# A recurrent attention with memory beside plain attention, on one core: the recurrence's value projection in four column tiles, its late rows in one early batch, its softmax sums by a matmul of ones and ln/exp

## The chip, the cores and the metric

The kernel runs on one core of a Trainium2 chip. The metric is the device time of one execution in microseconds (us). TensorE (PE) does the matmuls, VectorE (DVE) and ScalarE (ACT) the element-wise work, GpSimd (POOL) helps, SyncE (SP) issues DMAs.

## The reference

Two branches read the same x (2048 rows of 576) and are mixed by a gate. Branch A is a recurrence over 64 segments of 32 rows: 8 memory rows and 32 rows of x form h (40 rows); the memory rows of the output are the memory of the next segment. Branch B is full attention over all 2048 rows with 32 heads of 18.

```python
# A: 32 heads of 128, M = 8 memory rows, seg = 32, L = 40
mem = mem0
for s in range(64):
    h = concatenate([mem, x[:, s*32:(s+1)*32]], axis=1)       # 40 x 576
    q, k, v = h@Wq, h@Wk, h@Wv                                # 32 heads x 40 x 128
    p = softmax(where(mask, q@k.T * scale, -1e9))             # mask: key is memory, or not later
    o = (p @ v) @ Wo                                          # 40 x 576
    mem, a[s] = o[:, :8], o[:, 8:]
# B: plain softmax attention over 2048 rows, 32 heads of 18, then @ wo
g = sigmoid((x * gate_w).sum(-1))
out = g * a + (1 - g) * b
```

## The kernel before

**Opening.** x is loaded, transposed to `xT`, and B's queries, keys and values are projected (L164, L183) and written to DRAM. Then the weights of A are loaded: `wq`, `wk`, `wv` (4096 columns in five chunks of rows of Dm, the fifth padded with zeros) and `wo`.

**Recurrence.** Each segment does the following, in this order of dependence: x of the segment is transposed (L336) into columns 8 to 39 of `ht`; Q and K are projected head by head, five 128x40 matmuls each (`proj_T`, L351, 160 for Q and 160 for K); V in eight banks of 512 columns, five matmuls each (`v_part`, L371, 40 in all, 40 useful rows of a 128-wide stationary); scores with a mask matmul (L393, L402) and exp on ScalarE (L409); the row sums by 32 one-column matmuls (L417), reciprocal, a diagonal matrix (L425) and 32 matmuls that spread it (L436), and the multiplication (L443); then values times probabilities (L454), the output projection of 160 matmuls (L470, tile `pbw`), two casts that put the new memory in `ht_next` (L482, L483), and the transposed output (L491).

**Branch B fills in.** `b_steps` yields 512 steps, one per group of four heads, query block of 512 and key block of 128. A step is four score matmuls (L255, tile `sb`, each in its own 32-row tile of the array), two exps of 128x1024 on ScalarE (L267, `etb`), and four value matmuls (L270, tile `ob`, each in its own 32-column tile). `b_advance(per_seg)` adds 8 steps after each segment; a scheduler places the instructions on each engine in a fixed order, and each engine then runs its own in that order. PSUM holds three one-bank buffers that all of A's tiles share in turn (tag `pb`), two two-bank buffers for `sb` and one for `ob`.

**Closing.** b's output projection, the gate and the sum, 16 blocks of 128 rows (L525 to L543).

## Time and profile before

| what | value |
|---|---|
| median of 3 runs | 3181.43 us (3160.13 to 3200.14) |
| the profiled execution | 3178.58 us, its span 3176.8 us |
| PE busy | 3024.0 us, 95% of the span |
| ACT busy | 1481.7 us, 47% |
| DVE busy | 813.6 us, 26% |
| mean granted TensorE clock | 0.826 |

A busy PE is not a PE at its peak: a row of matmuls counts as busy from the first start to the last end. What one matmul costs in a run of them is read from start to start in a list in order of time.

### The profile page before, as it was taken

Reading aid. Unit: us, or ns where it says so; the run is one execution under the profiler, and the core shown is the slowest. Engines: PE = TensorE matmul, PEld = TensorE weight load, DVE = VectorE, ACT = ScalarE, POOL = GpSimd, SP = SyncE. Lnnn points to the kernel's source line nnn. Section 1 sums busy time; section 2 is a strip of 40 time slices with the busy share of each in tenths; the row PEclk is TensorE's granted clock in tenths of the full one; section 3 lists DMA queues with packets and bytes.
Section 4 is the critical chain, followed back from the end, with each engine's and each line's share of the span. In section 5 each row is a group of like instructions: output and inputs, shape, how many; then the busy total and the mean of one; then the engine's idle time right before and its main releaser. Section 6 shows DMA issues by size and latency. Waiting matters only on the chain.

```text
span 3176.8 us, 101992 instructions
## 1 busy us (share of the span) xinstructions
PE 3024.0 (95%) x47622; PEld 1807.9 (57%) x47765; DVE 813.6 (26%) x1664; ACT 1481.7 (47%) x2206; POOL 33.7 (1%) x144
## 2 busy tenths in 40 slices
PE   6789999999999999999999999999999999999996
PEld 3446555566556556555555655566565656565653
DVE  5312222222222222122222212222222222222214
ACT  2353445454544554454545445454544454445440
POOL 0100000000000000000000000000000000000000
PEclk9868887898879888787878878798888888788878
DMA  5640000000000000000000000000000000000004
GB/s 120 174 185 4 6 6 25 5 4 6 5 24 6 6 6 25 4 6 5 5 26 6 5 4 6 24 6 6 5 25 3 6 5 6 24 6 6 5 3 124
DMA packets 91117, 73.60 MB, mean 23 GB/s; under 512 B 63676, under 2 KB 82820, under 8 KB 88964
## 3 DMA queue, kind: packets, MB, share of 16 engines
q1 hardware_dynamic: 62210, 54.16, 5.5%
q10 hardware_dynamic: 28482, 12.90, 1.7%
q8 instruction: 373, 6.11, 0.8%
q14 instruction: 52, 0.43, 0.0%
HBM read 45.54 MB, written 21.50 MB: 21 GB/s over the span
## 4 chain that ended last, share of the span: by engine, by line
PE 88%; ACT 6%; DMA 3%; DVE 1%; issue 1%; ACTq 0%; SPq 0%; DVEq 0%
PE pb L351 19%; PE pvv L371 18%; PE ob L270 13%; PE sb L255 13%; PE pbw L470 11%; ACT etb L267 5%; PE pso L454 3%; PE psh L393 3%; PE psn L436 3%; PE psh L402 2%; PE pq L164 2%; PE psums L417 1%; DMA otn<-otd 1%; DMA wq<-in_A_Wq_dram 1%; PE po L525 1%
## 5 line engine op out<-in xcount | busy, mean ns | idle before, releaser
L267 ACT ACTIVATE etb<-sb 128x1024 bf16<-128x1024 f32 x1024 | 1011.0, 1024 | 385.2 <-PE sb L255 370.3
L371 PE MATMUL pvv<-wv,ht 128*128 128x512 bf16 x2432 | 583.3, 386 | 7.4 <-issue 1.2
L270 PE MATMUL ob<-etb,vgi 128*32 128x512 bf16 x2048 | 527.3, 471 | 55.0 <-ACT etb L267 49.4
L255 PE MATMUL sb<-qtg,ktg 18*128 18x512 bf16 x2048 | 537.4, 465 | 0.0
L351 PEld LDWEIGHTS <-wq 128*128 128x128 bf16 x10240 | 315.5, 99 | 185.8 <-issue 185.8
L371 PEld LDWEIGHTS <-ht 128*128 128x128 bf16 x2560 | 243.1, 99 | 287.7 <-issue 26.0
L351 PE MATMUL pb<-ht,wq 128*128 128x40 bf16 x10240 | 382.2, 185 | 15.4 <-DMA wq<-in_A_Wq_dram 15.4
L381 ACT CAST v_sb<-pvv 40x512 bf16<-40x512 f32 x256 | 148.0, 578 | 509.7 <-PE pvv L371 509.7
L470 PEld LDWEIGHTS <-wo 128*128 128x128 bf16 x10240 | 336.8, 109 | 39.1 <-issue 34.5
L470 PE MATMUL pbw<-qt_sb,wo 128*128 128x40 bf16 x10240 | 352.1, 195 | 0.0
L379 DVE CAST v_sb<-pvv 40x512 bf16<-40x512 f32 x256 | 174.8, 683 | 445.3 <-PE pvv L371 445.3
L351 PEld LDWEIGHTS <-wk 128*128 128x128 bf16 x10240 | 268.7, 96 | 15.2
L351 PE MATMUL pb<-ht,wk 128*128 128x40 bf16 x10240 | 269.6, 180 | 0.1
L255 PEld LDWEIGHTS <-ktg 18*128 18x128 bf16 x2048 | 106.9, 94 | 264.7 <-issue 255.7
L361 DVE CAST qt_sb<-pb 128x320 bf16<-128x320 f32 x128 | 62.9, 492 | 623.2 <-PE pb L351 617.4
L270 PEld LDWEIGHTS <-vgi 128*32 128x32 bf16 x2048 | 121.6, 95 | 168.9 <-issue 122.8
L486 ACT CAST ots<-pbw 128x128 bf16<-128x128 f32 x64 | 17.0, 265 | 311.6 <-DVE ht L483 251.3
L443 DVE TENSOR_TENSOR kt_sb<-psn,kt_sb 40x320 bf16<-40x320 f32 x256 | 111.8, 475 | 73.1 <-PE psn L436 72.6
L409 ACT ACTIVATE kt_sb<-psh 40x320 bf16<-40x320 f32 x256 | 110.0, 430 | 40.0 <-PE psh L402 16.5
L361 DVE CAST kt_sb<-pb 128x320 bf16<-128x320 f32 x128 | 62.9, 492 | 253.1 <-PE pb L351 253.1
L454 PEld LDWEIGHTS <-v_sb 40*128 40x128 bf16 x2048 | 79.8, 107 | 75.9 <-issue 75.0
L363 ACT CAST kt_sb<-pb 128x320 bf16<-128x320 f32 x128 | 54.4, 425 | 129.9 <-PE pb L351 129.9
(81 smaller groups left out, 1638.9 us busy)
## 6 DMA issues: line engine op xcount, KB each, us to landing
wo<-in_A_Wo_dram SPq DMA_DIRECT2D x1, 4608.0 KB
qtd<-stg SPq DMA_DIRECT2D x8, 512.0 KB, 4.3
qtg<-qtd SPq DMA_DIRECT2D x8, 512.0 KB, 3.6
ktd<-stg SPq DMA_DIRECT2D x8, 512.0 KB, 4.4
vgd<-vg ACTq DMA_DIRECT2D x8, 512.0 KB, 3.5
ktg<-ktd SPq DMA_DIRECT2D x8, 512.0 KB, 4.8
vgi<-vgd SPq DMA_DIRECT2D x8, 512.0 KB, 4.9
wq<-in_A_Wq_dram SPq DMA_DIRECT2D x1, 4096.0 KB
```

What stands on the lines that cost most here:

```text
L255: nc.tensor.matmul(sb[:, i, :], lhsT=ktg[32 * j:32 * j + DhB, kb * P:(kb + 1) * P], rhs=qtg[32 * j:32 * j + DhB, qc * QC:(qc + 1) * QC], s ...
L267: nc.scalar.activation(out=etb[:, :, :], in_=sbs[jp][:, :, :], func=ACT.Exp, scale=scale_b)
L270: nc.tensor.matmul(ob[32 * j:32 * j + 32, :], lhsT=vg[:, kb * P + 32 * j:kb * P + 32 * j + 32], rhs=ets[j // 2][:, j % 2, :], start=(kb == 0),
L351: nc.tensor.matmul(pb[:, 64 * j:64 * j + L], lhsT=w_tile[0:cz, c, h * Dh:(h + 1) * Dh], rhs=ht[0:cz, c, :], start=(c == 0), stop=(c == NC ...
L361: nc.vector.tensor_copy(out=dst, in_=src)
L371: nc.tensor.matmul(ph[:, 0:512], lhsT=ht_flat[0:cz, L * c:L * c + P], rhs=wv[0:cz, c, q8 * qcols:(q8 + 1) * qcols], start=(c == 0), stop=( ...
L379: nc.vector.tensor_copy(out=v_sb[0:L, q8 * qcols:(q8 + 1) * qcols], in_=ph[0:L, :])
L381: nc.scalar.copy(out=v_sb[0:L, q8 * qcols:(q8 + 1) * qcols], in_=ph[0:L, :])
L409: nc.scalar.activation(out=vw(et[0:L, HS * h0:HS * (h0 + 8)], HS, L), in_=vw(psh[0:L, :], 64, L), func=ACT.Exp, scale=scale_a,)
L443: nc.vector.tensor_tensor(out=vw(et[0:L, HS * h0:HS * (h0 + 8)], HS, L), in0=vw(psn[0:L, :], 64, L), in1=vw(et[0:L, HS * h0:HS * (h0 + 8)] ...
L454: nc.tensor.matmul(pso[:, 64 * j:64 * j + L], lhsT=v_sb[0:L, h * Dh:(h + 1) * Dh], rhs=et[0:L, HS * h:HS * h + L], start=True, stop=True,)
L470: nc.tensor.matmul(pbwv[0:cz, c, 0:L], lhsT=wo[:, h, c * P:c * P + cz], rhs=ot_sb[:, HS * h:HS * h + L], start=(h == 0), stop=(h == H - 1),)
```

## The change

The kernel computes the same and its tiling of B and its closing stay. What is different:

- **Values.** Of the 40 rows of V, the first 32 are computed in the segment, by 40 matmuls with a 32-column stationary and 512 moving columns, four of which (j = 0 to 3) write to four different 32-partition strips of one bank (L403). Two casts to `vm` and four DMAs bring them to `v_sb`. The last 8 rows of all 64 segments depend on x alone: they are computed in the opening in one batch (L248, 160 matmuls), go to DRAM (`vld`), and each segment loads its 8 rows (L389).
- **Q and K.** 576 is four chunks of 128 and a half one of 64. The half chunks of two heads share one 128-row stationary, so 16 matmuls of 80 columns (L430) take the place of 32 of 40, and 128 of 40 columns stay (L421). Banks hold 12, 12 and 8 heads.
- **Softmax.** The mask is a minimum with `cap` on VectorE (L458) behind the exp. One matmul of ones per bank sums and spreads in one (L465); ln (L476) and exp of its negative (L478) on ScalarE make the reciprocal, and VectorE multiplies it with `pso` (L479). Stationaries are padded to 128 rows and columns.
- **x.** Transposed once, in the opening, written to DRAM (`xtd`), loaded four segments at a time, copied on POOL (L380). The outputs are transposed every fourth segment.
- **B.** The four `ob` matmuls are held together (`issue_behind`), its loads go to POOL's queue. The weights of A are loaded during the opening. One activation table is named at the top (L75).

```diff
+    with tc.high_priority():
+        nc.scalar.preload_act_table_set("natural_log_exp_and_others")
...
+        SG = P // LO
+        for q in range(n_seg // SG):
+            vl = pw.tile([P, HD], BF16, name="vl")
+            for b in range(HD // 512):
+                pv = ps_q.tile([P, 512], FP32, name="pq")
+                for c in range(NF + 1):
+                    cc = c if c < NF else (NF if b < 4 else NF + 1)
+                    nc.tensor.matmul(
+                        pv[:, :],
+                        lhsT=xL[:, cc, q * P:(q + 1) * P],
...
-                    for j in range(4):
-                        nc.tensor.matmul(
+                    last = None
+                    for j in (2, 3, 0, 1):
+                        mm = nc.tensor.matmul(
...
+                        if last is not None:
+                            issue_behind(mm, last)
+                        last = mm
...
+            for c in range(NF + 1):
+                for j in range(4):
+                    f0 = j * 1024 + hf * 512
+                    if c < NF:
+                        lw, rw = ht[:, c, 0:CT], wv_m[:, c, f0:f0 + 512]
+                    else:
+                        f1 = f0 % (HD // 2)
+                        lw, rw = ht[:, NF + j // 2, 0:CT], wv_t[:, f1:f1 + 512]
+                    nc.tensor.matmul(
+                        pv[32 * j:32 * j + 32, :],
+                        lhsT=lw,
+                        rhs=rw,
+                        start=(c == 0),
+                        stop=(c == NF),
+                        tile_position=(0, 32 * j),
+                    )
+            nc.vector.tensor_copy(out=vm[:, hf * 512:(hf + 1) * 512], in_=pv[:, :])
+        for j in range(4):
+            nc.sync.dma_start(out=v_sb[0:CT, j * 1024:(j + 1) * 1024], in_=vm[32 * j:32 * j + 32, :])
...
+                    if h % 2:
+                        nc.tensor.matmul(
+                            pb[:, o - L:o + L].rearrange("p (a t) -> p a t", t=L),
+                            lhsT=w_t[:, h // 2, :],
+                            rhs=ht[:, NF:NF + 2, :],
+                            start=False,
+                            stop=(h == h0 + nh - 1),
+                            skip_group_check=True,
+                        )
...
+            nc.tensor.matmul(pss[:, 0:w], lhsT=ones[:, :], rhs=et[:, h0 * L:h0 * L + w], start=True, stop=True)
+            pso = ps_a.tile([P, 512], FP32, name="pso", tag="pb")
...
+            nc.scalar.activation(out=lns[:, 0:w], in_=pss[:, 0:w], func=ACT.Ln)
+            rcp = seg2.tile([P, 512], FP32, name="rcp")
+            nc.scalar.activation(out=rcp[:, 0:w], in_=lns[:, 0:w], func=ACT.Exp, scale=-1.0)
+            nc.vector.tensor_tensor(out=ot[:, h0 * L:h0 * L + w], in0=pso[:, 0:w], in1=rcp[:, 0:w], op=ALU.mult)
```

**How it moves instructions.** ScalarE, the stretch of one segment from the scores to the output projection. Before (`kt_sb` from `psh` is the exp, `etb` is B's exp, x4 means four in a row):

```order
L381 CAST v_sb<-pvv 40x512 x2
L409 ACTIVATE kt_sb<-psh 40x320 x4
L267 ACTIVATE etb<-sb 128x1024 x4
L462 CAST qt_sb<-pso 128x320
L267 ACTIVATE etb<-sb 128x1024
L462 CAST qt_sb<-pso 128x320
L267 ACTIVATE etb<-sb 128x1024
L486 CAST ots<-pbw 128x128
```

With the change (one whole segment):

```order
L456 ACTIVATE et<-psh 40x480 x2
L456 ACTIVATE et<-psh 40x320
L476 ACTIVATE lns<-pss 128x480
L304 ACTIVATE etb<-sb 128x1024
L478 ACTIVATE rcp<-lns 128x480
L476 ACTIVATE lns<-pss 128x480
L304 ACTIVATE etb<-sb 128x1024
L478 ACTIVATE rcp<-lns 128x480
L476 ACTIVATE lns<-pss 128x320
L304 ACTIVATE etb<-sb 128x1024
L478 ACTIVATE rcp<-lns 128x320
L304 ACTIVATE etb<-sb 128x1024 x13
```

Ln, B's exp and the exp of the reciprocal follow each other once per bank, so that three of B's sixteen exps of a segment lie between the ln and the exp of the reciprocal; thirteen follow, and all copies out of PSUM have left this engine.

TensorE, around the values' matmuls of one segment. Before, a run of 20 stands between the last matmul of Q and the first of K, a second one behind K:

```order
L351 MATMUL pb<-ht,wq 128x40
L371 LDWEIGHTS ht
L371 MATMUL pvv<-wv,ht 128x512
...
L371 MATMUL pvv<-wv,ht 128x512
L351 LDWEIGHTS wk
L351 MATMUL pb<-ht,wk 128x40
```

With the change the 40 stand ahead of Q, in seven runs (9, 6, 2, 8, 1, 11 and 3) between B's matmuls. One of the short runs:

```order
L308 LDWEIGHTS vgi
L308 MATMUL ob<-etb,vgi 32x512
L292 LDWEIGHTS ktg
L292 MATMUL sb<-qtg,ktg 128x512
L292 LDWEIGHTS ktg
L292 MATMUL sb<-qtg,ktg 128x512
L403 LDWEIGHTS ht_1423
L403 MATMUL pvv<-wv_m,ht_1423 32x512
L403 LDWEIGHTS ht_1423
L403 MATMUL pvv<-wv_t,ht_1423 32x512
L292 LDWEIGHTS ktg
L292 MATMUL sb<-qtg,ktg 128x512
```

From the end of the output projection to the last of B's matmuls there are, in nearly every segment, 7 runs of four `ob`, 10 runs of two or four `sb` (24 matmuls), the 40 of the values and 78 of Q; the other 66 of Q and all 144 of K follow with nothing of B between, and then the scores.

## Rows read from the trace of the kernel before

**Rows 1.** The page: the span, and the granted clock in 40 slices.

```profile
span 3176.8 us, 101992 instructions
PEclk9868887898879888787878878798888888788878
```

**Rows 2.** The page: the chain that ended last, by engine and by line.

```profile
PE 88%; ACT 6%; DMA 3%; DVE 1%; issue 1%; ACTq 0%; SPq 0%; DVEq 0%
PE pb L351 19%; PE pvv L371 18%; PE ob L270 13%; PE sb L255 13%; PE pbw L470 11%; ACT etb L267 5%; PE pso L454 3%; PE psh L393 3%; PE psn L436 3%; PE psh L402 2%; PE pq L164 2%; PE psums L417 1%; DMA otn<-otd 1%; DMA wq<-in_A_Wq_dram 1%; PE po L525 1%
```

**Rows 3.** Stretches: from:to, length, busy us of each engine, PEclk, DMA share, GB/s.

```profile
180.00:200.00 20.00, 18.16 (x69) 4.17 (x66) 0.00 (x0) 17.49 (x18) 0.00 (x0) 0.50 0.75 277
230.00:3109.00 2879.00, 2808.32 (x45534) 1696.83 (x45658) 704.77 (x1446) 1391.17 (x1994) 20.09 (x122) 0.82 0.03 9
1639.30:1663.00 23.70, 23.18 (x218) 9.42 (x218) 1.94 (x6) 13.82 (x15) 0.00 (x0) 0.50 0.02 4
2792.00:2804.60 12.60, 12.28 (x215) 7.16 (x213) 1.90 (x7) 10.20 (x13) 0.00 (x0) 1.00 0.03 8
2804.60:2817.40 12.80, 12.69 (x206) 7.87 (x203) 3.71 (x6) 3.01 (x6) 0.00 (x0) 1.00 0.01 3
2817.40:2837.00 19.60, 19.38 (x290) 11.44 (x290) 6.67 (x12) 9.18 (x13) 0.33 (x2) 0.57 0.03 8
```

**Rows 4.** TensorE in order of time, full clock: start us, length us, engine, line, what.

```profile
2792.00 0.40 PE L270 MATMUL ob<-etb,vgi 128*32 128x512 bf16 x3
2792.33 0.39 PE L255 MATMUL sb<-qtg,ktg 18*128 18x512 bf16 x4
...
2795.16 0.39 PE L255 MATMUL sb<-qtg,ktg 18*128 18x512 bf16 x2
2795.48 0.95 PE L351 MATMUL pb<-ht,wq 128*128 128x40 bf16 x31
...
2804.62 4.48 PE L371 MATMUL pvv<-wv,ht 128*128 128x512 bf16 x19
2808.94 4.21 PE L351 MATMUL pb<-ht,wk 128*128 128x40 bf16 x160
```

**Rows 5.** TensorE in order of time, half clock (the 144 see it rise).

```profile
186.38 0.61 PE L255 MATMUL sb<-qtg,ktg 18*128 18x512 bf16 x2
186.92 0.61 PE L270 MATMUL ob<-etb,vgi 128*32 128x512 bf16 x2
...
2786.89 0.61 PE L270 MATMUL ob<-etb,vgi 128*32 128x512 bf16 x1
2787.43 4.64 PE L470 MATMUL pbw<-qt_sb,wo 128*128 128x40 bf16 x144
```

**Rows 6.** Groups by line: count | busy us, mean ns of one | idle before.

```profile
L267 ACT ACTIVATE etb<-sb 128x1024 bf16<-128x1024 f32 x1024 | 1011.0, 1024 | 385.2 <-PE sb L255 370.3 <-DMA xseg<-in_A_x_dram 7.4 <-DVE ht L342 1.0
L409 ACT ACTIVATE kt_sb<-psh 40x320 bf16<-40x320 f32 x256 | 110.0, 430 | 40.0 <-PE psh L402 16.5
L174 ACT CAST stg<-pq 128x512 bf16<-128x512 f32 x32 | 18.7, 585 | 52.0 <-PE pq L164 36.2 <-DMA wvg<-in_B_wqkv_dram 7.8 <-DMA wqp<-in_B_wqkv_dram 4.7
L285 DVE TENSOR_TENSOR tn<-tq,rtb 128x512 bf16<-128x512 f32 x32 | 21.8, 682 | 0.0
L443 DVE TENSOR_TENSOR kt_sb<-psn,kt_sb 40x320 bf16<-40x320 f32 x256 | 111.8, 475 | 73.1 <-PE psn L436 72.6
L482 DVE CAST ht<-pbw 128x32 bf16<-128x32 f32 x63 | 12.1, 192 | 350.6 <-PE pbw L470 350.6
L483 DVE CAST ht<-pbw 64x8 bf16<-64x8 f32 x63 | 9.3, 148 | 0.2 <-issue 0.2
```

**Rows 7.** TensorE in order of time: the end of the opening, and the last segment's.

```profile
130.20 4.48 PE L164 MATMUL pq<-xT,wkp 128*128 128x512 bf16 x20
134.51 2.95 PE L183 MATMUL pq<-wvg,xT 128*128 128x72 bf16 x80
...
3108.44 5.98 PE L470 MATMUL pbw<-qt_sb,wo 128*128 128x40 bf16 x160
3114.78 0.53 PE L491 MATMUL pto<-ident,ots 128*32 128x128 bf16 x5 [0.35 <-ACT ots L486]
```

More of the change, by code (lines that the diff above doesn't have):

```diff
@@ L212 @@
+    aw2 = wctx.enter_context(tc.tile_pool(name="aw2", bufs=1))
+    wo = aw2.tile([P, H, Dm], BF16, name="wo")
+    for q in range(4):
+        nc.sync.dma_start(out=wo[:, 8 * q:8 * q + 8, :], in_=A_Wo[8 * q:8 * q + 8].rearrange("h e d -> e h d"))
     actx = ExitStack()
-    htpool = actx.enter_context(tc.tile_pool(name="htpool", bufs=2))
-    segpool = actx.enter_context(tc.tile_pool(name="segpool", bufs=2))
-    sbig = actx.enter_context(tc.tile_pool(name="sbig", bufs=1))
+    fix = actx.enter_context(tc.tile_pool(name="fix", bufs=1))
@@ L313 @@
[L313 to L321 removed]
+    hts = []
@@ new lines @@
+    for i in range(2):
+        h_ = fix.tile([P, NF + 2, L], BF16, name=f"ht{i}")
+        nc.vector.memset(h_[:], 0.0)
+        hts.append(h_)
+    v_sb = fix.tile([P, HD], BF16, name="v_sb")
+    nc.gpsimd.memset(v_sb[:], 0.0)
+    et = fix.tile([P, H * L], BF16, name="et")
+    nc.gpsimd.memset(et[:], 0.0)
+    qt = fix.tile([P, H * L], BF16, name="qt")
+    kt = fix.tile([P, H * L + P - L], BF16, name="kt")
+    nc.vector.memset(kt[:, H * L:], 0.0)
+    ot = fix.tile([P, H * L], BF16, name="ot")
@@ new lines @@
+    m0 = seg2.tile([P, Dm], BF16, name="m0", bufs=1)
+    nc.sync.dma_start(out=m0[0:M, :], in_=A_mem0[0])
+    ptm = ps_a.tile([P, NF + 2, 32], BF16, name="ptm", tag="pb")
+    for c in range(NF):
+        nc.tensor.transpose(out=ptm[:, c, 0:M], in_=m0[0:M, c * P:(c + 1) * P], identity=ident[0:M, 0:M])
+    nc.tensor.transpose(out=ptm[0:TL, NF, 0:M], in_=m0[0:M, NF * P:Dm], identity=ident[0:M, 0:M])
+    nc.tensor.transpose(out=ptm[:, NF + 1, 0:M], in_=m0[0:M, T0:Dm], identity=ident[0:M, 0:M])
@@ L440 @@
+        proj(wq_m, wq_t, qt)
+        proj(wk_m, wk_t, kt)
+        if s + 1 < n_seg:
+            put_x(s + 1)
+        for h0, nh in BANKS:
+            psh = ps_a.tile([P, 512], FP32, name="psh", tag="pb")
+            for h in range(h0, h0 + nh):
+                nc.tensor.matmul(
+                    psh[:, (h - h0) * L:(h - h0 + 1) * L],
+                    lhsT=kt[:, h * L:h * L + P],
+                    rhs=qt[:, h * L:(h + 1) * L],
                     start=True,
@@ L460 @@
                 )
[L461 to L475 removed]
+            lns = seg2.tile([P, 512], FP32, name="lns")
@@ new lines @@
+            nc.scalar.activation(out=lns[:, 0:w], in_=pss[:, 0:w], func=ACT.Ln)
+            rcp = seg2.tile([P, 512], FP32, name="rcp")
+            nc.scalar.activation(out=rcp[:, 0:w], in_=lns[:, 0:w], func=ACT.Exp, scale=-1.0)
+            nc.vector.tensor_tensor(out=ot[:, h0 * L:h0 * L + w], in0=pso[:, 0:w], in1=rcp[:, 0:w], op=ALU.mult)
+        pbw = ps_a.tile([P, 512], FP32, name="pbw", tag="pb")
+        for h in range(H):
+            for c in range(NF + 1):
+                d0 = c * P if c < NF else T0
+                nc.tensor.matmul(
+                    pbw[:, c * L:(c + 1) * L],
+                    lhsT=wo[:, h, d0:d0 + P],
+                    rhs=ot[:, h * L:(h + 1) * L],
+                    start=(h == 0 and c == 0),
+                    stop=(h == H - 1 and c == NF),
+                    skip_group_check=True,
@@ new lines @@
+        if i4 == 0:
+            otsg = seg2.tile([P, NF + 1, P], BF16, name="otsg")
+        nc.vector.tensor_copy(out=otsg[:, :, i4 * seg:(i4 + 1) * seg], in_=pw3[:, :, M:L])
+        if i4 == 3:
+            pto = ps_a.tile([P, Dm], BF16, name="pto", tag="pb")
+            for c in range(NF + 1):
+                d0 = c * P if c < NF else T0
+                nc.tensor.transpose(out=pto[:, d0:d0 + P], in_=otsg[:, c, :], identity=ident[:, :])
+            oseg = seg2.tile([P, Dm], BF16, name="oseg")
+            nc.vector.tensor_copy(out=oseg[:, :], in_=pto[:, :])
+            nc.sync.dma_start(out=a_dram[(s - 3) * seg:(s + 1) * seg, :], in_=oseg[:, :])
@@ L513 @@
     for j in range(4):
[L514 removed]
+        nc.sync.dma_start(out=wop[32 * j:32 * j + DhB, :, :], in_=wo_v[j])
     for n in range(NT):
```

524 lines of the change are left out of this document (212 added, 312 removed).

## The prediction

> **What bounds the kernel now.** I read the page's chain of waits first: nearly nine tenths of the span end on TensorE, and its largest lines belong to the recurrence, Q and K with 19%, the values with 18% [rows 2]. B's matmuls are there with 26%, though B has no order of its own to keep: in the recurrence TensorE is short of time, not of work. The stretches say so too: from 230 to 3109 us it is busy for 2808 of 2879 us [rows 3], 45.0 us a segment. ScalarE is busy for half of that and becomes interesting only when TensorE gets less to do. The second thing to see is the granted clock, 0.82 over the recurrence [rows 3]. It has two levels, 1.2 and 2.4 GHz. In one segment it is full while Q, V and K run and falls to 0.57 on average in the softmax stretch, where matmuls are narrow and wait for other engines [rows 3]; it rises again in the dense output projection.
>
> Last, what a matmul costs from start to start. At full clock a 40-column one costs 25 ns in a dense run (160 end where the next run starts, 4.06 us later) and a 512-column one 216 ns (20 of them, one not recorded, in 4.32 us) [rows 4]. B's matmuls come in tiles of the array: a run of three `ob` takes 0.33 us to the next run's start, and of two `sb` 0.32 us [rows 4]; at half clock a run of one takes 0.54, a run of two the same [rows 5]. So what a run of up to three costs does not depend on how many there are. The 0.11 us over 216 ns is the price of changing the tiling.
>
> **The change, part by part**, for one segment.
>
> *Values.* 40 x 216 ns = 8.64 us go away [rows 4]. In come 40 matmuls in runs of 9, 6, 2, 8, 1, 11 and 3. If four neighbours share the array, these are 3+2+1+2+1+3+1 = 13 times 216 ns and seven changes of 0.11: 3.6 us, and 6.3 us at half clock (13 x 0.43 + 0.77). If none shared, it would be 40 x 216 ns + 0.8 = 9.4 us. The nearest row is the run of three in 0.33 us [rows 4], so I take 3.6.
>
> *B's own matmuls.* Four `ob` in one run instead of two runs saves 0.33 us per step [rows 4]; a step is now some 0.97 us of TensorE, and two exps of 0.987 us on ScalarE (1024 of them keep it busy for 1011 us [rows 6]). That makes ScalarE the slower of the two for B.
>
> *Q and K.* 32 matmuls of 80 columns take the place of 64 of 40. The nearest row is 72 columns, 80 in 2.95 us or 37 ns each [rows 7]; 40 ns, against 51 for two of 40: 0.35 us saved. The Trainium skill, "TensorE: Matmul & The Clock Gate", section "Back-to-back issue gap", gives some 81 ns for a weight load and a 128-column matmul in a stream; by that the pairing could lose up to 1 us a segment, 60 us in all. The row of 72 columns is nearer and speaks against it.
>
> *Softmax.* The mask matmuls, the 32 one-column sums, the 32 that spread the reciprocal and the diagonal go, the six-instruction ScalarE part comes. I walk through it in the order of ScalarE, from the first score matmul at 0. Twelve scores and their latency: the first exp starts at 0.5. An exp of 480 columns takes 0.56 us (430 ns at 320, 585 at 512 [rows 6]); the three end at 2.1. The minimum on VectorE, 384 columns between 0.15 and 0.48 us (the upper end is 320 columns out of PSUM [rows 6]); I take 0.45. Sums by 2.1. Then ln to 2.7, B's exp to 3.7, exp to 4.3; ln, B's exp, exp to 6.4; the third bank to 8.2. The multiplication takes 0.65 (682 ns at 512 [rows 6]): the second bank's ends at 7.15. The output projection cannot start before that, though its first bank is ready at 5: its tile is the third buffer behind the second `pso`, which this multiplication reads. TensorE idles for most of 2.3 to 7.15, so I expect half clock there, as now. 160 matmuls take 5.8 us at half clock from 3108.44 on [rows 7] and 4.06 at full [rows 4]; a rise on the way, as now, gives 5.05. The stretch ends at **12.2 us** (11.3 at full clock).
>
> *The middle stretch.* 12 of B's exps follow, their first `sb` standing behind the output projection: 0.75 + 12 x 0.987 + 0.5 for the last `ob` = **13.05 us**. TensorE's own work there at full clock is 7 x 0.33 + 10 x 0.32 + 3.6 + 78 x 0.026 = 11.1 us: it waits for ScalarE. The casts of the memory (three of 0.15 to 0.19 us [rows 6]) hide behind the first `ob` and `sb`. At half clock it is 17 x 0.535 + 6.3 + 78 x 0.036 = 18.2, with the casts **18.5 us**, and TensorE bounds.
>
> *The tail.* 210 matmuls of Q and K with nothing beside them: 186 x 25 ns + 24 x 40 = **5.6 us**, 5.8 with some at half clock.
>
> *Hidden:* the values' DMAs (4 of 64 KB), with the rest of Q and K, some 8 us, between them and their reader; the load of eight rows; the copies on POOL; VectorE's casts, some 10 us of the segment in all. If the tail were shorter than the DMAs' way, the softmax would begin later by the rest.
>
> *Opening.* Q, K and V of B are 93 us now (320 x 216 ns and 8 x 2.95 us) and end at 137.5 [rows 7], so 44 us are loads and transposes. With the change: 320 x 216 ns = 69, V in 160 wider matmuls 20, the late values 160 x 216 ns = 35, and between 24 (smaller first loads) and 44 us ahead; I take 24: 148. B's first 8 steps, 16 us by ScalarE, and a tail bring the first scores to 170. The weights load meanwhile; now TensorE waits for them. *Closing:* the same code, 3114.4 to 3176.8, 62.4 us [rows 1, 7].
>
> **The sum.** 170 + 63 segments + 12.2 for the last one's softmax + 62.4. If the clock is full in three middle stretches of four, a segment is 12.2 + (0.75 x 13.05 + 0.25 x 18.5) + 5.8 = 32.4 us: 63 x 32.4 = 2041, in all 2286 us, and with the 2 us by which the profiled execution's time exceeds its span, **2290 us**. That execution, 3178.6 us, lies 0.1% below the median of the runs. The quarter is from now: at 0.82 the clock is half for 16 us of a segment, and the softmax with the output projection accounts for some 12; the rest are segments as at 1639 us, where the clock fell at the handover and stayed low for 23.7 us of Q and B [rows 3].
>
> **The rivals.**
>
> *Half clock in every middle stretch.* Speaking for it: at 180 to 200 us B's matmuls alone keep TensorE 91% busy at 0.50 [rows 3], and the middle stretch now waits for ScalarE. Against: the dense output projection stands right before it, and today's mixture of B and Q holds 1.00 from 2792 to 2804.6 [rows 3]. A segment is 12.9 + 18.5 + 7 = 38.4 us at most, the tail at half clock throughout, and 37.4 with a rise in it: **2600 to 2665 us**. The Trainium skill, "TensorE: Matmul & The Clock Gate", section "Why this matters for your kernels", warns of idle stretches between bursts, since the clock then falls back; by it this is the likelier case. 25%.
>
> *Full clock nearly everywhere*, the output projection too: 11.3 + 13.05 + 5.6 = 30.0, in all **2135 us**. For it: padded stationaries and no one-column matmuls. Against: the idle 5 us. 20%.
>
> *Slower.* The four strips run one after the other, at half clock and with a change each, as a lone `ob` does in 0.54 us [rows 5]: 40 x 0.54 = 21.4 instead of 6.3 makes the middle stretch 33.6 and a segment 53: **3570 us**. It decides from 46.6 us a segment. The run of three speaks against it. 2%.
>
> The forecast's own case (2200 to 2450) has 48%; 5% is for a kernel shorter than 2100, were the wait for the third buffer to cost less. A segment that gains nothing would need TensorE to be bound by something not seen here; that the change does not do what it says is excluded by the order of instructions.
>
> **The range.** 2110 to 2630 us: it takes in the full-clock case and the lower half of the half-clock case, and leaves out the upper half of that, the shorter kernel and the slower one, together 2 in 10. 2% is about what a measurement tells from no change. Faster by more: 0.97; within: 0.01; slower: 0.02.
>
> **What would show it.** Values: the span from the first to the last `pvv` follows B's exps, and a run of 9 takes 0.76 us at full clock. ScalarE: 21 us busy per segment, without idle time in the middle stretch and idle for the 5.6 us of the tail. `pbw` starts some 7 us behind the first `psh`, released by VectorE's second multiplication. Granted clock: near 0.8 in the recurrence; 0.6 would mean the half-clock rival, above 0.9 the other. A ScalarE that is idle in the middle stretch while TensorE is busy would prove the bound wrong; so would a wait of `pso` for a DMA.

## The result and the profile after

The changed kernel takes **2182.51 us** (median of 4 runs, 2182.30 to 2186.98); the kernel before took 3188.58 us beside it. The ratio is 0.686, with a 95% interval of 0.681 to 0.691. The forecast was 2290 us, with a range of 2110 to 2630.

From the page of the changed kernel: the span, the engines' busy time, the granted clock, and the chain by engine and by line. They answer to [rows 1, 2].

```profile
span 2180.6 us, 87040 instructions
PE 1994.0 (91%) x40694; PEld 1320.7 (61%) x40694; DVE 715.5 (33%) x1449; ACT 1266.8 (58%) x1698; POOL 62.7 (3%) x138
PEclk8898898999999999998989999999999999999989
...
PE 53%; ACT 35%; issue 6%; DMA 4%; DVE 1%; SPq 1%; ACTq 0%; POOL 0%; DVEq 0%
ACT etb L304 29%; PE pb L421 15%; PE pbw L484 15%; PE sb L292 5%; PE ob L308 4%; PE pb L430 3%; PE pq L197 3%; ACT et L456 2%; PE psh L448 2%; ACT lns L476 2%; PE pq L248 2%; PE pvv L403 2%; ACT rcp L478 1%; DMA otn<-otd 1%; PE po L535 1%
```

The chain that was 88% TensorE is now shared: B's exps end 29% of the span, the values 2% instead of 18%. The clock digits have risen from 8 and 7 to 9.

Stretches of the changed kernel (columns as in [rows 3]): the recurrence; a wait in the opening; then one segment's softmax, projection, middle and tail.

```profile
170.00:2110.00 1940.00, 1826.11 (x39480) 1232.22 (x39479) 624.90 (x1298) 1224.61 (x1603) 39.44 (x90) 0.92 0.10 30
61.00:79.80 18.80, 0.04 (x1) 0.04 (x1) 0.66 (x2) 0.68 (x2) 0.49 (x1) 0.57 1.09 334
1187.48:1193.74 6.26, 5.37 (x85) 3.07 (x82) 2.44 (x6) 5.61 (x11) 0.35 (x1) 0.97 0.04 13
1193.74:1198.66 4.92, 4.92 (x166) 4.88 (x164) 0.81 (x2) 2.14 (x3) 0.00 (x0) 0.69 0.02 3
1198.66:1211.20 12.54, 11.99 (x170) 5.50 (x171) 2.90 (x7) 11.32 (x12) 0.00 (x0) 1.00 0.09 22
1211.20:1216.75 5.55, 5.55 (x215) 5.55 (x212) 2.46 (x4) 0.00 (x0) 0.00 (x0) 1.00 0.02 6
```

The middle row is the one to see: TensorE is busy for 11.99 of 12.54 us, ScalarE for 11.32, and the clock is full. Both engines are nearly full there. What is left of the half clock lies around the output projection (0.69), from the end of the softmax on.

That segment in order of time, TensorE, ScalarE and VectorE.

```profile
1192.01 0.30 PE L465 MATMUL pss<-et,ones 128*128 128x320 bf16 x1 [0.56 <-ACT lns L476]
1192.92 0.40 PE L308 MATMUL ob<-etb,vgi 128*32 128x512 bf16 x4 [0.33 <-ACT etb L304]
1193.23 0.46 ACT L476 ACTIVATE lns<-pss 128x320 f32<-128x320 f32 x1
1193.26 0.52 PE L292 MATMUL sb<-qtg,ktg 18*128 18x512 bf16 x2
1193.40 0.66 DVE L479 TENSOR_TENSOR ot<-pso,rcp 128x480 bf16<-128x480 f32 x1 [1.21 <-ACT rcp L478]
1193.74 4.91 PE L484 MATMUL pbw<-ot,wo 128*128 128x40 bf16 x160
...
1199.24 0.82 PE L403 MATMUL pvv<-wv_m,ht 128*32 128x512 bf16 x9
1199.35 11.47 ACT L304 ACTIVATE etb<-sb 128x1024 bf16<-128x1024 f32 x12 [3.47 <-PE sb L292]
...
1206.79 0.20 PE L430 MATMUL pb<-ht,wq_t 128*128 128x80 bf16 x1
1206.83 0.35 PE L421 MATMUL pb<-ht,wq_m 128*128 128x40 bf16 x8
```

Twelve exps in a row take 11.47 us, 0.956 each. Nine values end within 0.82 us. A matmul of 80 columns, which serves the half chunks of two heads, is followed by the next one some 40 ns later.

Where the 16 us of a segment come from, added up over all matmuls of 63 segments (each from its start to the next one's; "waiting" is the time in which the trace shows TensorE idle), in us:

```
               values   ob    sb   Q,K  projection scores sums outputs transposes waiting  segment
before           8.85  6.94  7.24  9.24       5.36   2.49 2.31    1.40       0.85    1.12    45.80
changed          3.36  2.87  5.81  8.15       5.02   1.00 0.75    1.16       0.09    1.62    29.84
```

The values give 5.5 us and B's own matmuls (`ob` and `sb`) 5.5, the softmax's small ones (scores, sums, outputs) 3.3, Q and K 1.1. Part of each is the clock: 16.2 us of a segment ran at half clock before, 4.8 do now. What that is worth is an estimate: a 40-column matmul takes 25 ns at full clock and 36 at half (160 in 4.06 and in 5.8 us [rows 4, 7]), a 512-column one 216 and 425 (the fillers below), so 11.3 us less at half clock stand for 3.4 to 5.7 of the 16 us.

### The profile page after: what moved, and what is told of

It reads as the page before. It is cut to its first block, busy times and chain, and to the rows that moved or that the text cites. A ratio compares the mean times of both kernels' runs of the same rounds, so it can differ in the third digit from the quotient of the medians.

```text
span 2180.6 us, 87040 instructions
## 1 busy us (share of the span) xinstructions
PE 1994.0 (91%) x40694; PEld 1320.7 (61%) x40694; DVE 715.5 (33%) x1449; ACT 1266.8 (58%) x1698; POOL 62.7 (3%) x138
## 4 chain that ended last, share of the span: by engine, by line
PE 53%; ACT 35%; issue 6%; DMA 4%; DVE 1%; SPq 1%; ACTq 0%; POOL 0%; DVEq 0%
ACT etb L304 29%; PE pb L421 15%; PE pbw L484 15%; PE sb L292 5%; PE ob L308 4%; PE pb L430 3%; PE pq L197 3%; ACT et L456 2%; PE psh L448 2%; ACT lns L476 2%; PE pq L248 2%; PE pvv L403 2%; ACT rcp L478 1%; DMA otn<-otd 1%; PE po L535 1%
## 5 line engine op out<-in xcount | busy, mean ns | idle before, releaser
L484 PE MATMUL pbw<-ot,wo 128*128 128x40 bf16 x10240 | 326.1, 195 | 5.6 <-ACT lns L476 2.2
L421 PEld LDWEIGHTS <-wq_m 128*128 128x128 bf16 x8192 | 260.4, 96 | 67.8 <-issue 67.8
L421 PE MATMUL pb<-ht,wq_m 128*128 128x40 bf16 x8192 | 293.3, 180 | 0.0
L421 PE MATMUL pb<-ht,wk_m 128*128 128x40 bf16 x8192 | 250.0, 179 | 0.0
L421 PEld LDWEIGHTS <-wk_m 128*128 128x128 bf16 x8192 | 245.3, 96 | 0.0
L308 PE MATMUL ob<-etb,vgi 128*32 128x512 bf16 x2048 | 218.6, 406 | 28.1 <-ACT etb L304 22.2
L403 PE MATMUL pvv<-wv_m,ht 128*32 128x512 bf16 x2048 | 228.8, 388 | 0.1
L438 DVE CAST qt<-pb 128x480 bf16<-128x480 f32 (+1 forms) x192 | 115.6, 602 | 293.0 <-PE pb L430 293.0
L430 PE MATMUL pb<-ht,wq_t 128*128 128x80 bf16 x1024 | 201.8, 197 | 0.0
L430 PE MATMUL pb<-ht,wk_t 128*128 128x80 bf16 x1024 | 201.2, 197 | 0.0
L479 DVE TENSOR_TENSOR ot<-pso,rcp 128x480 bf16<-128x480 f32 (+1 forms) x192 | 113.6, 594 | 172.2 <-ACT rcp L478 172.2
L403 PEld LDWEIGHTS <-ht 128*32 128x32 bf16 x2560 | 59.0, 94 | 111.0 <-issue 98.1
L478 ACT ACTIVATE rcp<-lns 128x480 f32<-128x480 f32 (+1 forms) x192 | 110.7, 576 | 0.3
```

Of the source, the lines that this page charges most:

```text
L308: mm = nc.tensor.matmul(ob[32 * j:32 * j + 32, :], lhsT=vg[:, kb * P + 32 * j:kb * P + 32 * j + 32], rhs=ets[j // 2][:, j % 2, :], start=( ...
L403: nc.tensor.matmul(pv[32 * j:32 * j + 32, :], lhsT=lw, rhs=rw, start=(c == 0), stop=(c == NF), tile_position=(0, 32 * j),)
L421: nc.tensor.matmul(pb[:, o:o + L], lhsT=w_m[:, c, h * Dh:(h + 1) * Dh], rhs=ht[:, c, :], start=(h == h0 and c == 0), stop=False, skip_grou ...
L430: nc.tensor.matmul(pb[:, o - L:o + L].rearrange("p (a t) -> p a t", t=L), lhsT=w_t[:, h // 2, :], rhs=ht[:, NF:NF + 2, :], start=False, st ...
L438: nc.vector.tensor_copy(out=dst[:, h0 * L:(h0 + nh) * L], in_=pb[:, 0:nh * L])
L478: nc.scalar.activation(out=rcp[:, 0:w], in_=lns[:, 0:w], func=ACT.Exp, scale=-1.0)
```

## The experiments

Stages of a segment in us, from the first score matmul: "softmax" goes to the first matmul of the output projection, "projection" to the end of its last, "middle" from there to the start of the last `ob` or `sb`, "tail" to the next scores. They are means of 63 segments of the profiled execution; the time is the median of the runs. Half clock is worked out from the clock changes in the trace.

```
                    time us   softmax  projection  middle   tail  segment  half clock
before              3188.58     12.66        6.21   13.26  13.67    45.80       16.15
changed             2182.51      6.43        5.12   12.43   5.86    29.84        4.82
strip by strip      2376.42      6.43        5.18   15.23   6.05    32.91        5.47
not padded          2182.20      5.24        5.23   13.53   5.70    29.70        5.58
ob free             2230.56      6.29        4.79   13.29   6.28    30.65        3.36
half exps           2070.68      5.51        4.54    9.35   8.63    28.04        2.49
stores on ScalarE   2163.46      6.43        5.11   12.48   5.86    29.89        4.98
old sums            2329.95      9.93        5.08   10.84   6.40    32.25        9.16
values alone        2721.81     12.73        6.34   11.88   7.56    38.52       13.82
B behind Q          2254.23      6.96        5.13   17.41   1.34    30.84        7.64
double exps         2572.13     13.16        5.07   16.42   1.35    36.00       12.08
filler              2205.90      7.57        4.26   13.01   5.59    30.43        2.76
not paired          2220.70      6.48        5.24   12.47   6.29    30.48        5.74
projection by bank  2132.48      4.77        5.37   13.54   5.62    29.30        3.52
```

In "projection by bank" the projection holds the third bank's sums and outputs too. The runs come from five sittings, in which the kernel before took 3174 to 3202 us; the changed kernel was timed in one of them. So a difference of 1% or less is read from the stages and not from the time alone.

**Strip by strip.** Do the four strips share the array? Here the five chunks of one strip are written before those of the next.

```diff
-            for c in range(NF + 1):
-                for j in range(4):
+            for j in range(4):
+                for c in range(NF + 1):
```

> The changed kernel, with one alteration: the 40 value matmuls of a segment are written strip by strip (five chunks for one strip, then the next strip) instead of chunk by chunk, so that neighbours on TensorE lie in the same column tile. Work and bytes are the same. Theory: the values became cheap because four neighbours in four strips share the array. Then this kernel's values cost about 40 x 216 ns + 0.8 = 9.4 us of TensorE at full clock instead of 3.6, less what is shared where one strip ends and the next begins (some 6 of the 40): about 8 us. TensorE's own work in the middle stretch rises from about 11 to 15.5 us and passes ScalarE's 12.4, so a segment takes about 3 us longer than the 29.84 us of the changed kernel: 63 x 3 = 190 us, in all about 2370 us (2300 to 2430). Rival: neighbours cost the same wherever they lie and the middle stretch is set by ScalarE alone: no change, 2183 us within 1%.

2376.42 us (2372.01 to 2377.69), ratio to before 0.748 (0.744 to 0.752). The same 40 matmuls take 6.43 us instead of 3.36, and the segment grows by 3.07. A run in this kernel's order of time:

```profile
1200.73 1.05 PE L403 MATMUL pvv<-wv_m,ht 128*32 128x512 bf16 x7
1201.60 0.38 PE L403 MATMUL pvv<-wv_t,ht 128*32 128x512 bf16 x1
1201.91 0.39 PE L292 MATMUL sb<-qtg,ktg 18*128 18x512 bf16 x2
```

Eight end within 1.25 us here, nine within 0.82 in the changed kernel. Sharing is shown, and that it hangs on which matmuls are neighbours. The 40 cost less than the 8 us expected, because some still share: the eight shown take 1.18 us to the next run's start, less than eight times 216 ns.

**Values alone.** This is the kernel before with the values in four column tiles, now ahead of Q, and nothing else of the change; the values of the last 8 rows are left out.

```diff
+                        tile_position=(0, 32 * j),
...
+        v_part(0)
+        v_part(1)
...
-        for q8 in range(0, 4):
-            v_part(q8)
...
```

> The kernel before with one part of the change alone: the values of 32 of the 40 rows in four column tiles (40 matmuls, two copies of 128 rows and four DMAs into place, all before K). The values of the last 8 rows are left out (zero), so the output is not the reference's. Theory: values fall from 8.64 us to about 3.6 plus the changes of tiling; the tail and the softmax stay as they are, so a segment goes from 44.65 to about 39.5 us: 64 x 5 = 320 us, about 2860 us (2780 to 2930). Rival: what is saved is given back, since the dense 512-column matmuls that kept the clock up are gone and the clock is at half for more of Q and K: 2950 to 3180 us, with a granted clock below 0.82.

2721.81 us, ratio 0.855 (0.851 to 0.859), better than the theory's range: a segment loses 7.3 us, not 5. The values take 2.55 us instead of 8.85; Q and K, `sb` and waiting give another 1.2. The rival's clock did not come: it is 0.83 for the whole profiled execution, and 5 middle stretches of 63 have over 1 us of half clock where the kernel before had 13. This part is nearly half of the change's gain; the late rows that it leaves out cost the changed kernel 34.5 us, once, in the opening.

**Old sums.** This is the changed kernel with the kernel before's way to the row sums and the reciprocal.

```diff
-            pss = ps_a.tile([P, 512], FP32, name="pss", tag="pb")
-            nc.tensor.matmul(pss[:, 0:w], lhsT=ones[:, :], ...
...
+        nc.vector.reciprocal(out=rq[0:L, 0:H], in_=psums[0:L, 0:H])
...
+            nc.vector.tensor_copy(out=ot[:, h0 * L:h0 * L + w], in_=pso[:, 0:w])
```

> The changed kernel with the softmax's old way to its sums: 32 matmuls of one column, reciprocal, the diagonal, 32 matmuls that spread the reciprocal and three multiplications of the exponentials before the outputs, in place of the ones matmul, ln, exp and a multiplication of the outputs. Values, pairing and order of B stay as changed. Theory A, the clock follows how long TensorE waits in the softmax stretch: the chain from the first scores to the output projection grows from 6.5 to 11 to 13 us (12.75 in the kernel before), the granted clock falls in it and the projection goes back to 6.3 us, now and then the middle stretch too: 5.5 to 8 us a segment, less 0.6 to 3 us since ScalarE is spared six instructions and has more time for B's exps beside the wait: 2330 to 2650 us, most likely 2450. Theory B, the clock is kept by the values and B's batched matmuls, not by the shorter softmax: the chain alone costs 3 to 4 us net, the projection stays at 5 us: 2370 to 2430 us with the granted clock still at 0.9 or above.

2329.95 us (2328.22 to 2334.58): the softmax is 3.5 us longer, the middle and tail 1.1 shorter. That is 2.4 us net, a little less than either theory had. The chain in this kernel's order of time:

```profile
1268.84 0.65 PE L466 MATMUL psums<-ones,et 40*40 40x1 bf16 x20
1269.53 0.35 DVE L467 RECIPROCAL rq<-psums 40x32 f32<-40x32 f32 x1 [0.60 <-PE psums L466]
1269.91 1.48 DVE L468 TENSOR_TENSOR diag<-ident,rq 40x1280 bf16<-40x1280 bf16 x1
1271.45 1.01 PE L478 MATMUL psn<-diag,ones 40*40 40x40 bf16 x32 [0.26 <-DVE diag L468]
1271.94 1.61 DVE L479 TENSOR_TENSOR et<-psn,et 40x480 bf16<-40x480 f32 x3 [0.55 <-PE psn L478]
```

Half clock goes from 4.8 to 9.2 us a segment, nearly all of the rise in the softmax. The projection stays at 5.1 us and the middle at full clock in all 63 segments: what the clock has gained there over the kernel before does not come from the new sums.

**Half exps.** Half of B's exponentials are left out, and the `ob` matmuls read the other half twice.

```diff
-                        nc.scalar.activation(out=etb[:, :, :], in_=sbs[jp][:, :, :], func=ACT.Exp, scale=scale_b)
+                        nc.scalar.activation(out=etb[:, 0, :], in_=sbs[jp][:, 0, :], func=ACT.Exp, scale=scale_b)
...
-                            rhs=ets[j // 2][:, j % 2, :],
+                            rhs=ets[j // 2][:, 0, :],
```

> The changed kernel, with half of B's exponentials left out: each of its exps takes 512 columns instead of 1024, and the ob matmuls read that half twice (so B's outputs are not the reference's). TensorE's work is the same. Theory: ScalarE's exps of 0.987 us set the pace of the middle stretch (12 of them between the output projection and the tail). With exps of about 0.57 us TensorE sets it: its own work there is some 11 us by the sum that went into the prediction, so the stretch falls from 12.4 to about 11 us, and the softmax stretch by 2 x 0.42 us since two of B's exps lie between its own: 2.2 us a segment, 140 us in all, about 2040 us (2000 to 2080). Rival: TensorE sets the middle stretch already, and only the softmax stretch gains: 0.8 us a segment, about 2130 us.

2070.68 us (2066.04 to 2073.70). The size was right and the place was not: middle and tail together fall from 18.29 to 17.98 us only, softmax and projection by 1.5. ScalarE is now busy for 12.7 us a segment instead of 19.1. All of Q and K stand in the tail, none in the middle stretch, and the two stretches together still take nearly as long: it is TensorE's work that fills them. So ScalarE did not bound the middle stretch alone. In the changed kernel the two engines are balanced there, since the scheduler had drawn some of Q's matmuls, 78 in most segments, into the gaps.

The projection waits for no exp of B; it gains by the clock. Half clock in softmax and projection falls from 4.8 to 1.7 us. Why the clock stays up longer is not shown.

**Double exps.** Each of B's exps is done twice.

```diff
+                        nc.scalar.activation(out=etb[:, :, :], in_=sbs[jp][:, :, :], func=ACT.Exp, scale=scale_b)
```

> The changed kernel with each of B's exponentials done twice (the second writes the same values again), so that ScalarE's work for B doubles and TensorE's stays. It asks what the granted clock does in the middle stretch when TensorE has to wait there. In the changed kernel TensorE waits for about 0.4 us of 12.4 in that stretch and the clock is at 2.4 GHz in all 63 of them. ScalarE now has 16 x 2 x 0.99 + 5.2 = 36.8 us of work a segment, and with what it idles in the tail a segment takes 38 to 43 us. Theory A, it is this waiting that drops the clock, and the changed kernel stayed high because its planner had filled the waits with Q's matmuls: the clock is at half in most of the middle stretches, granted clock of the recurrence 0.6 to 0.75; as ScalarE has the time, this costs little by itself: 2750 to 3050 us. Theory B, the dense output projection ahead of it keeps the clock up, waits of a microsecond in between do nothing: the middle stretches stay at full clock, granted clock 0.85 or more, 2690 to 2950 us.

2572.13 us (2568.90 to 2579.22), below both ranges: ScalarE has few gaps left and is busy for 33.4 of the 36.0 us of a segment. One segment's softmax, projection and middle (columns as in [rows 3]):

```profile
1378.47:1391.13 12.66, 8.04 (x96) 3.68 (x93) 2.70 (x6) 11.83 (x19) 0.35 (x1) 0.67 0.01 1
1391.13:1396.55 5.42, 5.42 (x160) 5.37 (x160) 0.49 (x1) 4.07 (x5) 0.00 (x0) 0.50 0.06 17
1396.55:1414.12 17.57, 15.93 (x372) 10.99 (x370) 5.36 (x11) 16.79 (x19) 0.00 (x0) 1.00 0.07 18
```

The middle stays at full clock in 62 of 63 segments, but it was no test of long waits: the scheduler put most of Q and K there (243 of 288 matmuls in most segments), and TensorE waits for 1.6 us only. In the softmax, where it waits for 4.6 of 12.7 us, the clock falls. What as much waiting would do in the middle stays open.

**Not padded.** Scores, sums and outputs use 40 rows or columns of the array instead of 128.

```diff
-                    lhsT=kt[:, h * L:h * L + P],
+                    lhsT=kt[:, h * L:h * L + L],
...
```

> The changed kernel, with the small matmuls of the softmax stretch cut back: scores with a stationary of 40 columns instead of 128, sums and outputs that contract over 40 rows instead of 128. Work and order stay the same, only how much of the array each matmul fills. Theory A, the padding keeps the clock up: with 40 rows or columns the granted clock falls in the softmax stretch as it did in the kernel before, the output projection and part of the middle stretch run at half clock, and a segment takes 2 to 5 us longer: 2310 to 2500 us. Theory B, the clock stays up because TensorE's idle time between bursts has become short: no change, 2183 us within 1%, granted clock in the recurrence still 0.92.

2182.20 us (2173.07 to 2190.78). The granted clock is a little lower, 0.892 to 0.902 in the four runs against 0.911 to 0.916, and half clock rises from 4.8 to 5.6 us a segment. All but one of the 63 middle stretches have at most 1 us of it, and the time is the same, so the padding is not what keeps the clock up there. The order moved as well (one step's `ob` and two `sb` went behind the projection), so softmax and middle trade some 1.1 us, and the small fall of the clock cannot be put down to the padding alone.

**Filler.** Four matmuls of 512 columns that compute nothing of use stand ahead of the last eight outputs. The stores are moved as in the run on ScalarE's queue below, so it is compared with that one.

```diff
+            if h0 == 24:
+                for k in range(4):
+                    nc.tensor.matmul(pso[:, :], lhsT=ones[:, :], rhs=wv_m[:, k, 0:512], start=True, stop=True)
```

> The changed kernel with Q's and K's stores on ScalarE's queue (2163 us by itself), and four matmuls of 512 columns that compute nothing of use in each softmax stretch, ahead of the last eight outputs (they write to the tile that these then overwrite). They cost 4 x 216 ns = 0.86 us of TensorE a segment, some of it in time in which it waits. It asks whether the half clock in the output projection (3.7 of its 5.1 us in the changed kernel) can be bought off. Theory A: the clock falls for lack of work in the softmax stretch; with this work it falls later or not at all, the projection takes 4.2 to 4.6 us and a segment 0 to 0.5 us less: 2130 to 2163 us. Theory B: the clock falls at the same place, because the matmuls come too late or are too few: 0.5 to 0.9 us a segment more, 2195 to 2220 us.

2205.90 us (2204.74 to 2210.05) against 2163.46. Softmax and projection of one segment, columns as in [rows 3]:

```profile
1189.45:1197.31 7.86, 7.07 (x88) 3.64 (x85) 3.10 (x7) 6.84 (x12) 0.35 (x1) 0.78 0.01 2
1197.31:1201.42 4.11, 4.11 (x161) 4.08 (x161) 0.15 (x1) 0.00 (x0) 0.00 (x0) 1.00 0.05 20
```

The fillers themselves (one of the four has no record), and what follows them:

```profile
1194.21 0.62 PE L469 MATMUL pso<-wv_m,ones 128*128 128x512 bf16 x1
1195.06 1.06 PE L469 MATMUL pso<-wv_m,ones 128*128 128x512 bf16 x2 [0.22 <-issue]
1195.91 0.47 PE L471 MATMUL pso<-et,v_sb 128*128 128x40 bf16 x8
```

Both theories are half right. The clock is full in the projection (59 of 63 have at most 1 us at half), which takes 4.26 us instead of 5.11. But in the segment shown it fell ahead of the fillers: four take 1.70 us from the first start to the outputs, half-clock pace, and on average the softmax is longer by 1.14 us. The middle is 0.5 us longer too, with one `sb` more in it.

The segments differ. In 33 of 63 the clock is at half when the first filler starts, in 18 it falls during the fillers, and in 12 it holds. In those 12 the fillers take 0.86 us and the segment 29.41, 0.5 less than without them, as theory A had it; in the other 51 it takes 30.67. So four such matmuls in this place do not pay, since most come too late. Earlier ones were not tried.

**ob free.** The four `ob` matmuls of a step are no longer held together.

```diff
-                    for j in (2, 3, 0, 1):
+                    for j in range(4):
...
-                        if last is not None:
-                            issue_behind(mm, last)
```

> The changed kernel without the forced order of its four ob matmuls per step of B: the added dependency is left out and the heads are taken as 0, 1, 2, 3, so that they issue in two runs of two, each behind its own exp, with other matmuls between. Theory: a run of up to four costs the same, so two runs cost 0.33 us more of TensorE per step, 8 steps or 2.6 us a segment. In the middle stretch TensorE has some 1.3 us of slack against ScalarE, and 5 to 6 of the 8 steps lie there: a segment grows by 0 to 1.5 us, in all 2183 to 2280 us, most likely 2220. Rival: an ob that may go as soon as its own exp is done is never late, and TensorE was waiting anyway: no change or some 10 us less.

2230.56 us (2223.54 to 2235.75), inside the theory's range: `ob` takes 5.20 instead of 2.87 us a segment. The values give 0.6 of it back and the projection 0.3, and a segment grows by 0.8.

**Not paired.** Each matmul of 80 columns is written as two of 40.

```diff
-                            rhs=ht[:, NF:NF + 2, :],
...
+                        for a in range(2):
...
+                                rhs=ht[:, NF + a, :],
```

> The changed kernel with the pairing undone: each of the 32 matmuls of 80 columns that serve the half chunks of two heads is written as two of 40 columns, each with a weight load of its own. Theory: a pair costs some 35 ns from start to start (24 of them in a tail of 210 matmuls that takes 5.54 us, with 25.3 ns for each of the others) and two of 40 columns cost 51: 32 x 16 ns = 0.5 us a segment on TensorE, of which most lies in the tail with nothing beside it: 2200 to 2215 us. Rival: a wide matmul in such a run costs as much as two narrow ones, and the pairing bought nothing: 2183 us within 0.3%.

2220.70 us (2218.78 to 2228.37), a little above the theory's range: 0.64 us a segment, 0.46 of it Q and K themselves. The rival, no change, is excluded.

**Stores on ScalarE's queue.** B's Q and K are stored to DRAM by another engine's queue than the one that loads A's weights.

```diff
-                nc.sync.dma_start(out=dstd[g], in_=stg[:, :])
+                nc.scalar.dma_start(out=dstd[g], in_=stg[:, :])
```

> The changed kernel with one alteration in the opening: the stores of B's Q and K to DRAM are issued by ScalarE's queue instead of SyncE's, where they stand behind the loads of A's weights. Theory: TensorE's 18.8 us without work at 61 us, and part of the idle time around it, come from these stores, which cannot be issued until the weight loads ahead of them on SyncE have been; the staging buffers they read stay full, so VectorE and ScalarE cannot empty TensorE's results. Then the first scores come 15 to 35 us earlier than at 233 us, nothing else changes, and the time is 2147 to 2168 us. Rival: the transfers themselves are late because the weights take the bandwidth, and the queue does not matter: no change, 2183 us within 0.5%.

2163.46 us (2162.82 to 2165.89): the first scores come at 214.3 instead of 233.1 us, and a segment stays as it was (29.89 us). The wait that it removes, in the changed kernel's order of time:

```profile
63.10 8.58 SPq L120 DMA_DIRECT2D wk_t<-in_A_Wk_dram  x2
71.78 2.98 SPq L209 DMA_DIRECT2D qtd<-stg  x1
...
79.12 1.07 ACT L207 CAST stg<-pq 128x512 bf16<-128x512 f32 x2 [21.82 <-DMA qtd<-stg]
...
79.76 1.86 PE L197 MATMUL pq<-xT,wpk 128*128 128x512 bf16 x4 [18.76 <-ACT stg L207]
```

The store of Q stands behind the weight loads on SyncE; until it has landed ScalarE cannot reuse its buffer, and TensorE has nowhere to write.

**B behind Q.** Half of B's steps of a segment are moved behind the Q projection, so that some of its exps run beside K.

```diff
         proj(wq_m, wq_t, qt)
+        b_advance(per_seg // 2)
         proj(wk_m, wk_t, kt)
...
-        b_advance(per_seg)
+        b_advance(per_seg // 2)
```

> The changed kernel with B's steps of a segment written in two halves, four at the end of a segment as now and four behind the Q projection, so that B's exps also run beside K, in the tail where ScalarE is idle for 5.9 us. Theory: the middle stretch is held by ScalarE (12 exps in a row, TensorE a few tenths idle) and the tail by TensorE alone; spreading B evenly takes away the ScalarE bound, and what is left is TensorE's own work, at most some 0.6 us a segment less (that is what middle and tail gained when the exps were halved): 2140 to 2183 us. Rival: TensorE is short of work, not ScalarE, and more switches between the tilings of B and the projection cost 0.11 us each: 0 to 2 us a segment more, 2183 to 2310 us.

2254.23 us (2249.70 to 2266.76), on the rival's side, but not for its reason alone. Waiting grows from 1.6 to 2.1 us a segment and half clock from 4.8 to 7.6; 17 middle stretches of 63 have over 1 us of it, where the changed kernel had none. In the 46 whose middle stretch keeps the full clock, middle and tail take 18.08 us against 18.29, and the softmax 0.7 more. So using ScalarE's idle tail gains 0.2 us there, and spreading B costs more than that in the softmax and in clock.

**Projection by bank.** With the stores moved, the output projection of the first twelve heads stands ahead of the third bank's sums.

```diff
...
+            if h0 == 12:
+                pbw = ps_a.tile([P, 512], FP32, name="pbw", tag="pb")
+                out_proj(0, 12)
+            elif h0 == 24:
+                out_proj(12, 12)
+                out_proj(24, 8)
```

> The changed kernel with Q's and K's stores on ScalarE's queue (2163 us by itself) and the output projection written bank by bank: its matmuls for the first twelve heads stand behind the second bank's outputs, as soon as the first multiplication allows, instead of behind the last bank's. TensorE's order is then sums and outputs of two banks, 60 projection matmuls, sums and outputs of the last bank, 100 projection matmuls, with one step's ob and two sb moved from the softmax stretch to the middle one. Theory: the softmax stretch waits for the chain exp, ln, exp, multiplication, with TensorE idle for about 1.2 us and then at half clock in the projection (3.7 of 5.1 us); the 60 matmuls fill that wait, so the memory is ready at about 10.6 us from the first scores instead of 11.55, and the middle stretch gives back about half of it: 0.3 to 0.9 us a segment, 2105 to 2145 us. Rival: what the softmax stretch gains, the middle stretch pays, since ScalarE has done one or two of B's exps less by then and paces it: 2150 to 2230 us.

**2132.48 us** (2131.70 to 2147.16), ratio to before 0.673 (0.670 to 0.677): inside the theory's range, 31 us below the run with the stores alone, and the fastest here of those that leave nothing out. TensorE in its order of time:

```profile
1155.00 0.72 PE L292 MATMUL sb<-qtg,ktg 18*128 18x512 bf16 x3
1156.52 1.67 PE L466 MATMUL pbw<-ot,wo 128*128 128x40 bf16 x60 [0.80 <-DVE ot L491]
1158.04 0.30 PE L477 MATMUL pss<-et,ones 128*128 128x320 bf16 x1
1158.38 0.36 PE L480 MATMUL pso<-et,v_sb 128*128 128x40 bf16 x8
1158.58 2.66 PE L466 MATMUL pbw<-ot,wo 128*128 128x40 bf16 x100
```

The projection ends 10.14 us behind the first scores instead of 11.55, and the middle takes back 1.1. Half clock is 3.5 us a segment instead of 5.0.

**What the runs add up to.** Values alone gives 7.3 us a segment in the kernel before; in the changed kernel the new sums are worth 2.4, the `ob` matmuls held together 0.8 and the pairs 0.6. The rest of the 16 us, with the mask matmuls, the early transposes and the order of B's steps in it, no run isolates.

## Why the prediction was right

The time lies in the range and 4.7% below the point. The mechanism was right in the main: TensorE stays the engine that is short of time, the values share the array, and the softmax chain gets shorter. How near the time came to the point is in part luck. Its sum and what the trace says:

- **Opening, 170 forecast, 233 measured: the largest miss.** The first Q matmul starts at 23.5 us as taken, but Q and K need 114 us, not 69: 18.8 of waiting for the store, 19.9 for the rest of the transposes of x between them (9.3 us) and their waits, and 75.8 of their own. V takes 26.6 instead of 20. The step left out lies behind the late values: 9.8 us until B's first `sb`, 7 of them a wait for the load of K. "The weights load meanwhile" was true of TensorE's input and missed whose queue it held up; stores on ScalarE's queue shows it.
- **A segment, 32.4 forecast, 29.84 measured.** 1.36 of the 2.56 us are the quarter of middle stretches at half clock: none of 63 was. That quarter was read correctly from before (13 of 63 have over 1 us of half clock) and carried over wrongly: values alone brings it to 5. With B behind Q it is 17 again, so where B's steps and the values stand matters. What the clock answers to in this stretch stays open.
- Softmax, 7.15 to the projection's start, 6.43 measured. "The output projection cannot start before the second multiplication ends" is refuted: it starts at 1193.74, while that multiplication runs from 1193.40 to 1194.06. It followed ScalarE's third ln, over at 1193.69, and two `sb`; the profile shows no wait there for the multiplication. So its tile probably took the buffer of the third sums, which that ln had read, and not that of the second outputs. Projection, 5.05: 5.12 measured.
- Middle and tail at full clock, 18.85: 18.29. The exps are 0.956 us each in a row, not 0.987 (and the terms of the 13.05 add up to 13.09). "It waits for ScalarE" was too simple, as half exps shows: the sum had 26 ns for each Q matmul in the middle, but with the pairs and the changes of tiling the 78 of them take 2.67 us (34 ns each).
- Values, 3.6: 3.36, and sharing is shown by strip by strip. `ob`, 2.64 saved: 4.07, since the runs before were often at half clock; ob free isolates 2.3. Pairs, 0.35 saved: 0.64.
- The signs. ScalarE is busy for 19.1 us a segment, not 21. The granted clock of the recurrence is 0.92 and not near 0.8: by the prediction's own sign that is the full-clock rival's side.
- Closing, 74.6: 67.5.

So 63 us too little stand ahead of the recurrence, and 161 + 7 too much in and behind it: the errors have opposite signs, and without the one in the opening the time would have been some 2120 us.

*The rivals.* Half clock in every middle stretch did not come. The Trainium skill, "TensorE: Matmul & The Clock Gate", section "Why this matters for your kernels", warns of idle stretches between bursts, since the clock then falls back. The prediction took that to speak for this rival, but the middle stretch has hardly any idle time: TensorE is busy for 11.99 of 12.54 us. In every segment the clock fell 3.9 to 7.1 us behind the first scores, though no single wait in the softmax was above 0.90 us (0.56 in the segment shown); so a count of long waits alone would not have found it.

The Trainium skill, "TensorE: Matmul & The Clock Gate", section "Back-to-back issue gap", gives some 81 ns for a weight load and a 128-column matmul in a stream, by which the pairs might have lost. The trace has 35 ns for one of 80 columns (24 of them and 186 of 40 at 25.3 ns in the tail's 5.54 us), and not paired decides for the trace.

Full clock nearly everywhere (30.0 us a segment) was nearest for the segment, though the projection still runs largely at half (3.7 of 5.1 us).

## What to carry to other kernels

When one engine has all the work, look for matmuls that use a part of it: put into column tiles, narrow ones share the array if neighbours lie in different strips, and a run of up to four costs like one (0.33 us here, with the change of tiling). Before planning around a second engine's idle time, halve that engine's work in a run: here it showed that the first engine's work fills the stretch as well. Order may cost clock: compare the half clock of two runs before putting a difference down to work. In an opening, read for every store which queue it waits in and whose buffer it keeps.

## What the hardware showed that was not expected

Values and `ob` have the same tiling, and a change need not be paid between them. In the changed kernel eleven `pvv` from 1204.47 are followed by `ob` after 0.55 us, less than their own three rounds of 216 ns, so `ob` began in a strip that was free:

```profile
1204.47 0.82 PE L403 MATMUL pvv<-wv_m,ht 128*32 128x512 bf16 x10
1204.92 0.38 PE L403 MATMUL pvv<-wv_t,ht 128*32 128x512 bf16 x1
1205.02 0.49 PE L308 MATMUL ob<-etb,vgi 128*32 128x512 bf16 x4
```

In strip by strip they even alternate, and start within 0.03 us of each other:

```profile
1202.67 0.38 PE L308 MATMUL ob<-etb,vgi 128*32 128x512 bf16 x1
1202.68 0.38 PE L403 MATMUL pvv<-wv_m,ht 128*32 128x512 bf16 x1
1202.69 0.39 PE L308 MATMUL ob<-etb,vgi 128*32 128x512 bf16 x1
1202.70 0.58 PE L403 MATMUL pvv<-wv_m,ht 128*32 128x512 bf16 x2
```

The Trainium skill, "TensorEngine Tiling (Array Packing)", section "Key Properties", says that a change of mode drains the array and a change of tile does not; these rows agree. The prediction charged 0.11 us at the end of each of the seven runs.
